# Mish of a unit: one ScalarE instruction in place of sigmoid, tanh seed and one iteration, and the second product one unit sooner

## The chip, the cores and the metric

The kernel runs on one core of a Trainium2 chip. A core has TensorE (PE, with its weight loads shown apart as PEld), VectorE (DVE), ScalarE (ACT), GpSimd (POOL) and SyncE (SP, which issues the DMAs). Each engine takes its instructions in the order in which they were written. The metric is the device time of one execution in microseconds (us), as the median of three runs.

## The reference

Three layers run one after the other on 3072 tokens of width 384. The first is a delta-rule attention, a recurrence over 768 steps. The second is a dense layer of 2048 hidden units with Mish, and the third is a sum over 8 experts of 1024 hidden units, weighted by gates that eight rounds of normalising balance over all tokens.

```python
# attention, per head: y_t = q_t S;  S += beta_t k_t (v_t - S^T k_t)
x = attention(q, k, v, beta)                # 3072 x 384
h = x @ w_in                                # 384 -> 2048
x2 = (h * tanh(log1p(exp(h)))) @ w_out      # Mish, 2048 -> 384
P = balanced(exp(x2 @ w_gate))              # 3072 x 8, eight rounds
out = sum over e of P[:, e] * (relu(x2 @ w1[e]) @ w2[e])
```

## The kernel before, in words

The tokens are cut into six blocks of 512, numbered 0 to 5. After a start of about 111 us, in which the attention of block 0 runs almost alone, there is one window for each block: 16 Mish units (128 hidden units each, f = 0 to 15), then 8 units of the first expert (f = 16 to 23). Into window c is woven the attention of block c+1 (its matrix inverses, and a chain of 16 stages of small products with VectorE work between them) and the preparation of block c+2. After the last window come the other seven experts over all blocks, 336 units of TensorE work to the end of the program.

Every float32 product is made of three passes over a value split in a rounded high part and a low rest. A unit's first product is 9 matmuls into a PSUM bank (`m_first`; two banks of name `psh`). For a Mish unit, `m_a` starts the Mish, `m_b` ends it, `m_x` copies the unit's bank to SBUF (which frees the bank), `m_c` splits the result in `gh` (ScalarE) and `gl` (GpSimd), and `m_second` multiplies both with the second weights, 9 matmuls that add into three banks over all 16 units. `x2_done` reads these banks and splits them as the input of the expert units.

Before the change Mish is made as x (1 - r^2) / (1 + r^2) with r = 1 - sigmoid(x): a Sigmoid and a Tanh on ScalarE give a seed for a reciprocal, three VectorE operations and one of GpSimd prepare an iteration, a Square on ScalarE and two VectorE operations end it. At mark f of a window the code emits `m_first(f)`, `m_b(f-2)`, `m_a(f-1)`, `m_c(f-2)`, `m_x(f-1)`, then side stages, then `m_second(f-3)`; three more marks (f1 to f3) drain the last units, then `x2_done` follows. The two names `s` and `x` of the Mish have two buffers each, and so have `gh` and `gl`.

Side work has its own rules. The order is written out by hand (the table `PLACES` gives the marks). The steps of an inverse lie in a queue `eq` and are taken by VectorE a few at a time: after each VectorE call through the wrapper `vec` (line 461) as far as a credit allows, and by `fill(us)` at fixed places. In block 0 the weights of the Mish layer arrive as 64-bit floats and are decoded there: three VectorE operations a chunk (L191, L194, L199), then a copy on ScalarE (L254) and a subtraction on GpSimd (L255).

Of the kernel before, what the change touches and what calls it, by code (L numbers as in the profile page):

```python
# [8 lines left out]
F32 = mybir.dt.float32  # L9
# [3 lines left out]
AF = mybir.ActivationFunctionType  # L13
# [18 lines left out]
SEED_A, SEED_B = -2.0367336171479424, 0.7523828762448455  # L32
SEED_SHIFT, SEED_SCALE, SEED_ERR = -2.1307765265811733, -0.33690854580335866, 0.0073


def plan_chunks(uses, first, nslots, extra_at, nextra):
    """Which weight chunk goes to which slot, and at which unit it is loaded."""
# [49 lines left out]
def delta_mish_sinkhorn_kernel(  # L87
# [31 lines left out]
    neg3_sb = const.tile([128, 1], F32, name="neg3_sb")  # L119
# [41 lines left out]
    def fetch(i):  # L161
        """Brings a chunk as it is; the first ones of the mish block are 64 bits wide."""
# [20 lines left out]
    def queue_decode(i):  # L183
        """A float64 as a float32: its exponent 896 less, 24 bits of its fraction."""
# [27 lines left out]
    def fill_next():  # L212
        """One step of the side work on the vector engine: its cost, or None if none can be taken."""
        if not eq:
            return None
        cost, fn = eq.popleft()
        fn()
        return cost + 0.001
# [108 lines left out]
    # ================= balanced gates =================  # L327
# [48 lines left out]
    # ================= phase 1: attention and the mish block =================  # L376
# [4 lines left out]
    with ExitStack() as p1:  # L381
# [116 lines left out]
        def prep_ss(c, t):  # L498
            """The same on the scalar engine alone."""
# [12 lines left out]
        def prep_root(c):  # L512
            """Half the norms, from the scalar engine's table; root_ops makes them exact."""
            ss, ne, rn, bn = nrms[c % 2]
            nc.scalar.activation(out=ne, in_=ss, func=AF.Sqrt, scale=0.25)
# [308 lines left out]
        def m_a(u):  # L824
            i = u % 2
            s, p, f = mi_s[i], mi_m[i], mi_f[i]
            nc.scalar.activation(out=s, in_=hps[u], func=AF.Sigmoid)
            nc.scalar.activation(out=f, in_=s, func=AF.Tanh, scale=SEED_A, bias=seed_sb)
            vec.scalar_tensor_tensor(out=p, in0=s, scalar=-2.0, in1=s, op0=ALU.add, op1=ALU.mult)
            vec.tensor_scalar(out=f, in0=f, scalar1=SEED_SHIFT, scalar2=None, op0=ALU.add)  # L830
            vec.scalar_tensor_tensor(out=s, in0=p, scalar=2.0, in1=f, op0=ALU.add, op1=ALU.mult)
            nc.gpsimd.tensor_tensor(out=p, in0=p, in1=f, op=ALU.mult)  # L832

        def m_x(u):
            nc.scalar.activation(out=mi_x[u % 2], in_=hps.pop(u), func=AF.Copy)  # L835

        def m_b(u):
            i = u % 2
            s, p, x = mi_s[i], mi_m[i], mi_x[i]
            nc.scalar.activation(out=s, in_=s, func=AF.Square, scale=2.0 * SEED_SCALE, bias=neg3_sb)  # L840
            vec.scalar_tensor_tensor(
                out=p, in0=s, scalar=3.0 - 3.0 * SEED_ERR ** 2, in1=p, op0=ALU.add, op1=ALU.mult
            )
            vec.scalar_tensor_tensor(
                out=x, in0=p, scalar=-SEED_SCALE / (4.0 - 3.0 * SEED_ERR ** 2), in1=x, op0=ALU.mult, op1=ALU.mult
            )
# [48 lines left out]
        def warm(n, cols=512, i=0):  # L895
            """Keeps the tensor engine's clock up while it waits or its products fill few rows."""
# [13 lines left out]
        with tc.manual_schedule():  # L910
# [20 lines left out]
            nc.vector.memset(seed_sb, SEED_B)  # L931
            nc.vector.memset(half_sb, 0.5)
            nc.vector.memset(neg3_sb, -3.0)
# [30 lines left out]
            nc.scalar.activation(out=mi_s[0][:, 0:1], in_=seed_sb, func=AF.Sigmoid)  # L964
# [82 lines left out]
        def spread(first, last, n, total):  # L1047
            """Places for `total` stages, n at each mark from the first on, and the rest at the last."""
# [16 lines left out]
        def window(c):  # L1065
            """Side work of a window by its place: stages of the tensor engine, and the rest."""
# [46 lines left out]
        with tc.manual_schedule():  # L1113
            banks[:] = [0, [A1, A1]]
            for c in range(NBLK):
# [16 lines left out]
                for f in range(U1 + 3):  # L1132
# [5 lines left out]
                    if 2 <= f < U1 + 2:  # L1138
                        m_b(b + f - 2)
                    if 1 <= f <= U1:  # L1140
                        m_a(b + f - 1)
                    if 2 <= f < U1 + 2:
                        m_c(b + f - 2)
                    if 1 <= f <= U1:
                        m_x(b + f - 1)
# [6 lines left out]
                    if f == 2 or not c:  # L1152
                        banks[1] = [A1, A1, (ps_o1, "o3")]
                    side_rest(m, posts)
                    if 3 <= f:
                        m_second(b + f - 3)
# [7 lines left out]
                x2_done(c)  # L1164
                side_rest("f4", side_pe("f4", 0))
# [175 lines left out]
```

## Time and profile before

| | |
|---|---|
| median of three runs | 2471.75 us (2467.51 to 2473.41) |
| span of the profiled execution | 2464.6 us; no other total of it is shown |
| TensorE busy | 2313.3 us, 94% of the span |
| VectorE busy | 1170.0 us, 47% |
| ScalarE busy | 734.7 us, 30% |
| GpSimd busy | 601.6 us, 24% |
| windows of blocks 0 to 5 | 111.09 to 1047.20 us of the span |

Shares of busy time are means over the start, the windows and the seven experts, which have different limits; so they are read stage by stage. The median lies 7.15 us above the span.

### The profile page before, as it was taken

How to read it: one execution, taken by the hardware profiler on the slowest of the kernel's cores; microseconds unless marked ns; L12 is line 12 of the kernel's file. 1: busy time of each engine (PE TensorE's matmuls, PEld its weight loads, DVE VectorE, ACT ScalarE, POOL GpSimd, SP SyncE). 2: the span in 40 equal slices, each digit the busy share in tenths (PEclk: the TensorE clock that was granted, in tenths of full speed). 3: DMA queues.
4: the chain of work that ended last, by engine and by line, in shares of the span. 5: the costliest groups of instructions: out<-in, count | busy, mean ns of one | idle time of the engine just before them, and what ended most of it. 6: DMA issues, size and time to landing. Idle time of an engine off the chain costs nothing.

```text
span 2464.6 us, 36964 instructions
## 1 busy us (share of the span) xinstructions
PE 2313.3 (94%) x15492; PEld 1995.3 (81%) x15492; DVE 1170.0 (47%) x1850; ACT 734.7 (30%) x1286; POOL 601.6 (24%) x466
## 2 busy tenths in 40 slices
PE   5777989999999998899999999999999999999998
PEld 3556767877778786789999999999999999999998
DVE  8899597877878837642222222222222221222222
ACT  4254455353553535322121121121111112112111
POOL 4675736173460414231020020020001002001000
PEclk8778899999999999999999999999999999999999
DMA  5334752543634444341010010010001001000111
GB/s 166 132 128 151 203 192 105 195 144 142 192 109 168 142 169 164 109 160 39 1 52 1 1 52 1 1 40 13 1 19 34 1 1 52 1 1 26 26 23 29
DMA packets 79734, 196.06 MB, mean 80 GB/s; under 512 B 7696, under 2 KB 50448, under 8 KB 79568
## 3 DMA queue, kind: packets, MB, share of 16 engines
q1 hardware_dynamic: 79568, 193.70, 23.9%
q8 instruction: 122, 2.00, 0.3%
q14 instruction: 44, 0.36, 0.0%
HBM read 161.43 MB, written 32.24 MB: 79 GB/s over the span
## 4 chain that ended last, share of the span: by engine, by line
PE 69%; DVE 13%; POOL 7%; issue 6%; ACT 2%; DMA 1%; SPq 0%; POOLq 0%; DVEq 0%; ACTq 0%
PE psh L302 34%; PE o L324 29%; DVE p L461 3%; PE y L324 3%; POOL p L832 2%; POOL gl L853 2%; DVE x L461 2%; PE x L864 2%; DVE t L638 1%; DVE lane L644 1%; DVE lane L626 1%; POOL w L255 1%; DMA w<-wd 1%; DVE s L461 1%; PE psa L884 1%
## 5 line engine op out<-in xcount | busy, mean ns | idle before, releaser
L317 DVE SCALAR_TENSOR_TENSOR hl<-psh,hh 128x512 fp32r<-128x512 f32 x384 | 265.2, 691 | 1109.7 <-ACT hh L316 1109.6
L302 PE MATMUL psh<-xh,w 128*128 128x512 f32 x2052 | 674.0, 410 | 53.5 <-ACT x L835 29.6
L316 ACT ACTIVATE hh<-psh 128x512 fp32r<-128x512 f32 x384 | 229.7, 598 | 1314.9 <-PE o L324 1152.1
L302 PEld LDWEIGHTS psh<-xh,w 128*128 128x128 f32 x2052 | 387.3, 195 | 138.8 <-ACT x L835 38.0
L302 PE MATMUL psh<-xl,w 128*128 128x512 f32 x1026 | 416.9, 406 | 4.2 <-DVE xl L461 4.2
L324 PE MATMUL o<-w,hh 128*128 128x384 f32 x1584 | 405.3, 337 | 0.0
L324 PEld LDWEIGHTS o<-w,hh 128*128 128x128 f32 x1584 | 288.1, 188 | 19.9 <-issue 5.3
L324 PE MATMUL o<-wx,hh 128*128 128x384 f32 x1104 | 282.4, 336 | 0.0
L324 PE MATMUL o<-w,hl 128*128 128x384 f32 x792 | 266.8, 337 | 0.0
L302 PE MATMUL psh<-xh,wx 128*128 128x512 f32 x828 | 257.5, 392 | 0.0
L302 PEld LDWEIGHTS psh<-xl,w 128*128 128x128 f32 x1026 | 200.1, 195 | 52.0 <-DVE xl L461 6.8
L255 POOL TENSOR_TENSOR w<-raw,w 128x768 fp32r<-128x768 f32 x41 | 76.8, 1872 | 663.6 <-ACT w L254 658.4
L832 POOL TENSOR_TENSOR p<-p,f 128x512 f32<-128x512 f32 x96 | 113.5, 1182 | 446.0 <-DVE s L461 419.0
L324 PEld LDWEIGHTS o<-wx,hh 128*128 128x128 f32 x1104 | 201.7, 188 | 13.0 <-issue 2.2
L324 PE MATMUL o<-wx,hl 128*128 128x384 f32 x552 | 186.1, 337 | 0.0
L302 PEld LDWEIGHTS psh<-xh,wx 128*128 128x128 f32 x828 | 153.4, 188 | 25.0
L864 PE MATMUL x<-gh,w 128*128 128x512 f32 x576 | 157.0, 409 | 7.0 <-ACT gh L852 7.0
L302 PE MATMUL psh<-xl,wx 128*128 128x512 f32 x414 | 163.4, 395 | 0.0
L461 DVE SCALAR_TENSOR_TENSOR p<-s,p 128x512 f32<-128x512 f32 x96 | 122.8, 1279 | 81.2 <-ACT s L840 37.5
L324 PEld LDWEIGHTS o<-w,hl 128*128 128x128 f32 x792 | 148.6, 188 | 0.0
L864 PEld LDWEIGHTS x<-gh,w 128*128 128x128 f32 x576 | 111.6, 197 | 35.7 <-ACT gh L852 10.1
L255 POOL TENSOR_TENSOR wx<-raw,wx 128x768 fp32r<-128x768 f32 x23 | 42.5, 1849 | 398.5 <-ACT wx L254 398.5
(174 smaller groups left out, 3021.5 us busy)
## 6 DMA issues: line engine op xcount, KB each, us to landing
w<-wd SPq DMA_DIRECT2D x120, 768.0 KB, 4.3
raw<-in_w_dram SPq DMA_DIRECT2D x128, 192.0 KB, 2.6
wd<-w SPq DMA_DIRECT2D x24, 768.0 KB, 4.6
kq<-in_qkb_dram SPq DMA_DIRECT2D x20, 256.0 KB, 7.1
vt<-in_vtok_dram SPq DMA_DIRECT2D x6, 768.0 KB, 8.6
kq<-in_w_in_dram SPq DMA_DIRECT2D x12, 384.0 KB, 4.1
kq<-in_w_out_dram SPq DMA_DIRECT2D x12, 384.0 KB, 4.8
y0d<-xr SPq DMA_DIRECT2D x6, 768.0 KB, 4.1
```

The lines of the kernel that those rows point to most:

```text
L255: nc.gpsimd.tensor_tensor(out=w[:, 1], in0=r, in1=w[:, 0].bitcast(F32), op=ALU.subtract)
L302: mm(ps, lhsT=wi(u, pw, kc), rhs=(xh, xl)[px][:, kc, :], start=(n == 0), stop=(n == 3 * KD - 1))
L316: nc.scalar.activation(out=h, in_=ps, func=AF.Relu)
L317: nc.vector.scalar_tensor_tensor(out=l, in0=ps, scalar=0.0, in1=h.bitcast(F32), op0=ALU.max, op1=ALU.subtract)
L324: mm(o[t], lhsT=(h, l)[ph][:, t * 128:(t + 1) * 128], rhs=wo(u, pw, 0, DM), start=(f == 0 and n == 0), stop=(f == U2 - 1 and n == 2))
L461: f(*a, **k)
L626: + [(1.14, lambda p=p: nc.vector.transpose(out=lane[p:p + 32], in_=v[p:p + 32, 32:64, :])) for p in (32, 96)]
L638: eng[0].tensor_tensor(out=slot[0], in0=lane[:, s + 1:32, s:s + 1].to_broadcast([128, n, s]), in1=lane[:, s:s + 1, 0:s].to_broadcast([128, ...
L644: eng[0].tensor_tensor(out=lane[:, s + 1:32, 0:s], in0=lane[:, s + 1:32, 0:s], in1=slot[0], op=ALU.add)
L832: nc.gpsimd.tensor_tensor(out=p, in0=p, in1=f, op=ALU.mult)
L853: nc.gpsimd.tensor_tensor(out=l, in0=p, in1=h.bitcast(F32), op=ALU.subtract)
L864: mm(x2ps[c][k], lhsT=wo(u, pw, k * 128, k * 128 + 128), rhs=(h, l)[pg], start=(f == 0 and n == 0), stop=(f == U1 - 1 and n == 2))
```

## The change

`m_a` becomes one ScalarE instruction, Mish from the activation table, from the PSUM bank to SBUF; this read also frees the bank, so `m_x` goes, and `m_b` with it. `m_c` follows `m_a` at once, at the same mark. `m_second` is emitted two marks after `m_first`, not three, and `x2_done` moves from behind mark f3 to mark f2, ahead of the side stages of f2 and f3. Since fewer calls go through `vec`, a `fill(2.0)` is added at each mark and behind f4. One warming activation at the start loads the Mish table where it loaded that of Sigmoid.

```diff
         def m_a(u):
-            i = u % 2
-            s, p, f = mi_s[i], mi_m[i], mi_f[i]
-            nc.scalar.activation(out=s, in_=hps[u], func=AF.Sigmoid)
-            nc.scalar.activation(out=f, in_=s, func=AF.Tanh, scale=SEED_A, bias=seed_sb)
-            vec.scalar_tensor_tensor(out=p, in0=s, scalar=-2.0, in1=s, op0=ALU.add, op1=ALU.mult)
-            vec.tensor_scalar(out=f, in0=f, scalar1=SEED_SHIFT, scalar2=None, op0=ALU.add)
-            vec.scalar_tensor_tensor(out=s, in0=p, scalar=2.0, in1=f, op0=ALU.add, op1=ALU.mult)
-            nc.gpsimd.tensor_tensor(out=p, in0=p, in1=f, op=ALU.mult)
-
-        def m_x(u):
-            nc.scalar.activation(out=mi_x[u % 2], in_=hps.pop(u), func=AF.Copy)
-
-        def m_b(u):
...
-            nc.scalar.activation(out=s, in_=s, func=AF.Square, scale=2.0 * SEED_SCALE, bias=neg3_sb)
-            vec.scalar_tensor_tensor(
-                out=p, in0=s, scalar=3.0 - 3.0 * SEED_ERR ** 2, in1=p, op0=ALU.add, op1=ALU.mult
-            )
-            vec.scalar_tensor_tensor(
-                out=x, in0=p, scalar=-SEED_SCALE / (4.0 - 3.0 * SEED_ERR ** 2), in1=x, op0=ALU.mult, op1=ALU.mult
-            )
+            nc.scalar.activation(out=mi_x[u % 2], in_=hps.pop(u), func=AF.Mish)
...
-            nc.scalar.activation(out=mi_s[0][:, 0:1], in_=seed_sb, func=AF.Sigmoid)
+            nc.scalar.activation(out=mi_s[0][:, 0:1], in_=seed_sb, func=AF.Mish)
...
-                    if 2 <= f < U1 + 2:
-                        m_b(b + f - 2)
                     if 1 <= f <= U1:
                         m_a(b + f - 1)
-                    if 2 <= f < U1 + 2:
-                        m_c(b + f - 2)
-                    if 1 <= f <= U1:
-                        m_x(b + f - 1)
+                        m_c(b + f - 1)
...
+                    if f == U1 + 1:
+                        m_second(b + U1 - 1)
+                        x2_done(c)
                     side_rest(m, posts)
-                    if 3 <= f:
-                        m_second(b + f - 3)
+                    if 2 <= f <= U1:
+                        m_second(b + f - 2)
+                    fill(2.0)
...
-                x2_done(c)
                 side_rest("f4", side_pe("f4", 0))
+                fill(2.0)
```

Where the instructions stand is seen at three places. The first is TensorE at the start of block 5, in which no side work lies. L302 (L299 after the change) is a first product, and the number behind `w` is its weight slot; L864 (L840) is a second product into the banks `x`. Before, from the third unit of the block on:

```order
L302 MATMUL psh<-xh_1200,w_88 128x512 x2
L302 MATMUL psh<-xl_1201,w_88 128x512
...
L302 MATMUL psh<-xh_1200,w_89 128x512 x2
L302 MATMUL psh<-xl_1201,w_89 128x512
...
L864 MATMUL x_8636<-gh,w_86 128x512
L864 MATMUL x_8637<-gh,w_86 128x512
```

And with the change, from the same unit on:

```order
L299 MATMUL psh<-xh_1198,w_87 128x512 x2
L299 MATMUL psh<-xl_1199,w_87 128x512
...
L840 MATMUL x_7878<-gh,w_85 128x512
L840 MATMUL x_7879<-gh,w_85 128x512
...
L299 MATMUL psh<-xh_1198,w_88 128x512 x2
L299 MATMUL psh<-xl_1199,w_88 128x512
```

The second product of unit 0 (slot 86 before, 85 now) stood behind the first product of unit 3 and stands now behind that of unit 2.

The second place is ScalarE in block 5. Before, two units take these rows, where L827 is Sigmoid, L828 Tanh, L840 Square, L852 the split into `gh`, L835 the copy that frees the bank:

```order
L827 ACTIVATE s_172<-psh 128x512
L828 ACTIVATE f_178<-s_172,seed_sb 128x512
L852 ACTIVATE gh<-x_177 128x512
L835 ACTIVATE x_176<-psh 128x512
L840 ACTIVATE s_172<-s_172,neg_sb 128x512
L827 ACTIVATE s_173<-psh 128x512
```

Now the last units of block 5 read as follows, where L822 is Mish, L828 the split, L846 and L852 are `x2_done`, L313 is a Relu of an expert unit, and L344 the Sigmoid of the gates:

```order
L822 ACTIVATE x_175<-psh 128x512
L828 ACTIVATE gh<-x_175 128x512
L822 ACTIVATE x_176<-psh 128x512
L828 ACTIVATE gh<-x_176 128x512
L846 ACTIVATE xh_1198<-x_7878 128x512
...
L852 ACTIVATE xr<-x_7880 128x512
L313 ACTIVATE hh<-psh 128x512
L344 ACT_TABLE_LOAD
L344 ACTIVATE lg<-lg,gate 128x192
```

A unit has two ScalarE instructions, not five. The program before has three table loads, all in the start; the program after has the same three and this fourth, and none among the Mish units.

The third place is GpSimd in block 0, where it also prepares keys and values (L549, L563) and splits decoded weights (L255). Before, one mark of the block reads:

```order
L832 TENSOR_TENSOR p_175<-p_175,f_179 128x512
L853 TENSOR_TENSOR gl<-x_176,gh 128x512
L549 TENSOR_TENSOR vt_145<-vt_145,ne_153 128x384
L563 TENSOR_TENSOR kq_139<-kq_139,mask_sb 64x512
L255 TENSOR_TENSOR w_86<-kq_136,w_86 128x768
```

And with the change, the mark with the same work:

```order
L829 TENSOR_TENSOR gl<-x_176,gh 128x512
L546 TENSOR_TENSOR vt_144<-vt_144,ne_152 128x384
L560 TENSOR_TENSOR kq_138<-kq_138,mask_sb 64x512
L252 TENSOR_TENSOR w_85<-kq_135,w_85 128x768
L829 TENSOR_TENSOR gl<-x_175,gh 128x512
```

The product of the iteration (L832) is gone, the low part of a unit is made one mark sooner, and what else stands in the queue ahead of it stays.

## Rows read from the trace of the kernel before

**Rows 1.** The page, part 2: the span in 40 slices, tenths busy; granted clock.

```profile
DVE  8899597877878837642222222222222221222222
...
PEclk8778899999999999999999999999999999999999
```

**Rows 2.** Stretches: us, busy us and instructions of PE PEld DVE ACT POOL, PEclk, DMA, GB/s.

```profile
111.09:267.03 155.94, 117.42 (x1121) 90.01 (x1121) 141.30 (x159) 76.60 (x124) 102.34 (x76) 0.81 0.47 154
133.24:202.48 69.24, 50.39 (x557) 39.14 (x557) 67.96 (x69) 35.93 (x55) 44.88 (x29) 0.77 0.42 137
202.48:246.96 44.48, 36.84 (x411) 29.73 (x411) 42.55 (x50) 20.55 (x33) 27.10 (x17) 0.89 0.42 144
246.96:267.03 20.07, 15.37 (x49) 10.40 (x46) 13.78 (x17) 10.43 (x21) 12.78 (x9) 0.74 0.76 199
267.03:316.06 49.03, 47.34 (x321) 41.18 (x321) 29.75 (x63) 17.95 (x35) 30.81 (x30) 0.93 0.73 240
316.06:473.64 157.58, 140.02 (x1391) 115.15 (x1390) 130.61 (x235) 74.02 (x130) 69.20 (x57) 0.97 0.46 152
473.64:780.57 306.93, 284.60 (x2780) 233.40 (x2778) 249.13 (x418) 147.87 (x260) 138.03 (x114) 0.96 0.46 152
780.57:914.77 134.20, 130.57 (x1200) 107.67 (x1198) 90.96 (x125) 65.83 (x110) 39.14 (x32) 0.96 0.44 154
914.77:1005.16 90.39, 74.76 (x303) 55.35 (x302) 64.00 (x84) 50.79 (x85) 38.74 (x32) 0.98 0.45 158
1005.16:1047.20 42.04, 40.77 (x208) 35.23 (x209) 29.75 (x79) 10.16 (x18) 5.68 (x3) 0.96 0.25 85
1047.20:2464.60 1417.40, 1407.50 (x7061) 1271.81 (x7060) 337.51 (x542) 247.15 (x395) 115.47 (x58) 1.00 0.08 25
```

**Rows 3.** The same view of single units: block 4, block 5, and an expert unit.

```profile
847.77:853.17 5.40, 5.40 (x54) 4.31 (x50) 4.51 (x8) 3.17 (x5) 2.42 (x2) 1.00 0.41 149
965.95:971.26 5.31, 4.45 (x18) 3.30 (x18) 3.96 (x6) 3.05 (x5) 2.42 (x2) 1.00 0.48 148
894.79:898.95 4.16, 4.16 (x22) 3.79 (x22) 0.69 (x1) 0.60 (x1) 0.00 (x0) 1.00 0.51 189
```

**Rows 4.** Groups by line, whole run: busy us, mean ns, idle before and its releasers.

```profile
L461 DVE SCALAR_TENSOR_TENSOR p<-s,p 128x512 f32<-128x512 f32 x96 | 122.8, 1279 | 81.2 <-ACT s L840 37.5 <-POOL p L832 31.0 <-POOL kq L563 6.7
...
L461 DVE SCALAR_TENSOR_TENSOR x<-p,x 128x512 f32<-128x512 f32 x96 | 87.2, 909 | 3.2
...
L461 DVE SCALAR_TENSOR_TENSOR p<-s 128x512 f32<-128x512 f32 x96 | 78.2, 815 | 5.3 <-ACT s L827 5.3
...
L461 DVE SCALAR_TENSOR_TENSOR s<-p,f 128x512 f32<-128x512 f32 x96 | 66.4, 692 | 3.2
...
L827 ACT ACTIVATE s<-psh 128x512 f32<-128x512 f32 x96 | 56.7, 590 | 18.4 <-PE psh L302 17.5
...
L461 DVE TENSOR_SCALAR f<-f 128x512 f16<-128x512 f16 x96 | 29.0, 302 | 0.1
```

**Rows 5.** Timeline of VectorE (DVE) in block 0: start us, length us, instruction, idle before.

```profile
124.12 0.67 DVE L461 SCALAR_TENSOR_TENSOR p<-s,p 128x512 f32<-128x512 f32 x1
...
129.04 1.77 DVE L461 SCALAR_TENSOR_TENSOR p<-s,p 128x512 f32<-128x512 f32 x1 [1.85 <-POOL p L832]
```

**Rows 6.** Timeline of GpSimd (POOL) in the same stretch.

```profile
127.84 1.16 POOL L832 TENSOR_TENSOR p<-p,f 128x512 f32<-128x512 f32 x1
128.96 1.30 POOL L853 TENSOR_TENSOR gl<-x,gh 128x512 fp32r<-128x512 f32 x1
```

**Rows 7.** Timeline of ScalarE at the table load before the units.

```profile
21.05 1.28 ACT L964 ACT_TABLE_LOAD   x1
```

**Rows 8.** Timeline at the end of the Mish units of block 5.

```profile
1001.87 0.63 ACT L852 ACTIVATE gh<-x 128x512 fp32r<-128x512 f32 x1 [3.08 <-DVE x L461]
...
1002.55 1.66 PE L864 MATMUL x<-gh,w 128*128 128x512 f32 x6 [1.03 <-ACT gh L852]
...
1005.16 0.73 PE L302 MATMUL psh<-xh,w 128*128 128x512 f32 x2 [0.23 <-ACT xh L870]
```

More of the change, by code (lines that the diff above doesn't have):

```diff
@@ L31 @@
 ROUNDS = 8
-SEED_A, SEED_B = -2.0367336171479424, 0.7523828762448455
-SEED_SHIFT, SEED_SCALE, SEED_ERR = -2.1307765265811733, -0.33690854580335866, 0.0073
 def plan_chunks(uses, first, nslots, extra_at, nextra):
@@ L118, in delta_mish_sinkhorn_kernel @@
     seed_sb = const.tile([128, 1], F32, name="seed_sb")
-    neg3_sb = const.tile([128, 1], F32, name="neg3_sb")
     lg = const.tile([128, NT, E], F32, name="lg")
@@ L824, in m_a @@
         def m_a(u):
-            i = u % 2
-            s, p, f = mi_s[i], mi_m[i], mi_f[i]
-            nc.scalar.activation(out=s, in_=hps[u], func=AF.Sigmoid)
-            nc.scalar.activation(out=f, in_=s, func=AF.Tanh, scale=SEED_A, bias=seed_sb)
-            vec.scalar_tensor_tensor(out=p, in0=s, scalar=-2.0, in1=s, op0=ALU.add, op1=ALU.mult)
-            vec.tensor_scalar(out=f, in0=f, scalar1=SEED_SHIFT, scalar2=None, op0=ALU.add)
-            vec.scalar_tensor_tensor(out=s, in0=p, scalar=2.0, in1=f, op0=ALU.add, op1=ALU.mult)
-            nc.gpsimd.tensor_tensor(out=p, in0=p, in1=f, op=ALU.mult)
-        def m_x(u):
-            nc.scalar.activation(out=mi_x[u % 2], in_=hps.pop(u), func=AF.Copy)
-        def m_b(u):
-            i = u % 2
-            s, p, x = mi_s[i], mi_m[i], mi_x[i]
-            nc.scalar.activation(out=s, in_=s, func=AF.Square, scale=2.0 * SEED_SCALE, bias=neg3_sb)
-            vec.scalar_tensor_tensor(
-                out=p, in0=s, scalar=3.0 - 3.0 * SEED_ERR ** 2, in1=p, op0=ALU.add, op1=ALU.mult
-            )
-            vec.scalar_tensor_tensor(
-                out=x, in0=p, scalar=-SEED_SCALE / (4.0 - 3.0 * SEED_ERR ** 2), in1=x, op0=ALU.mult, op1=ALU.mult
-            )
+            nc.scalar.activation(out=mi_x[u % 2], in_=hps.pop(u), func=AF.Mish)
         def m_c(u):
@@ L930, in delta_mish_sinkhorn_kernel @@
             nc.gpsimd.memset(mi_f[1], 0.0)
-            nc.vector.memset(seed_sb, SEED_B)
+            nc.vector.memset(seed_sb, 0.0)
             nc.vector.memset(half_sb, 0.5)
-            nc.vector.memset(neg3_sb, -3.0)
             nc.vector.memset(sk["ones"], 1.0)
```

## The prediction

> **What bounds the kernel now.** I read the slices of the page first. VectorE is mostly at 7 to 9 tenths through the first sixteen slices and at 2 after the nineteenth, and the granted TensorE clock shows a 7 or an 8 only in the first five [rows 1]. So I cut the span at the starts of the blocks [rows 2]. From 1047.20 us on, in the other seven experts, TensorE is busy 1407.5 of 1417.4 us at full clock, and no edit touches that code; the start up to 111 us loses one memset. What can change lies in 936.1 us of windows, of which TensorE is busy 835.5. Its 100.6 us of idle time, and what it works at half clock, are the stock to gain from.
>
> The stock lies unevenly. In the Mish part of block 0 TensorE is idle 38.5 of 155.9 us at a granted clock of 0.81, while VectorE is busy 141.3. In block 5's Mish part it is idle 15.6 of 90.4, in block 1 17.6 of 157.6, in blocks 2 and 3 together 22.3 of 306.9, in block 4 only 3.6 of 134.2 [rows 2]. Single units say why. A unit of block 4 with one side stage takes 5.40 us without any idle time: TensorE is the bound. A bare unit of block 5 takes 5.31 us with 0.86 idle, and no engine is full: there the latency of the Mish is the bound. An expert unit, as many matmul columns, takes 4.16 [rows 3]. So a bare Mish unit needs about 4.35 of TensorE (4.45 less a little, since busy time counts waits inside a group), and a side stage 5.40 - 4.35 = 1.05.
>
> **What each edit costs or gives.** Five VectorE instructions go: 1279 + 909 + 815 + 692 + 302 ns = 4.0 us a unit, 384 us over 96 units [rows 4]. The GpSimd product of 1.16 us goes too [rows 6], and three ScalarE instructions. Mish itself has no row. The Sigmoid that reads the same bank at the same shape takes 590 ns [rows 4]; an activation of that shape lies between this and the 630 ns of the split into `gh` [rows 8], or higher if Mish needed more per element. I take 0.6. Even 1.2 would be less than what ScalarE loses, since that engine is busy only 3.05 of 5.31 us of a bare unit [rows 3].
>
> *Block 0, units 4 to 9.* They take 69.24 us, 11.5 each, with VectorE busy 67.96 [rows 2]. These busy times hold waiting. The same instruction takes 0.67 us alone [rows 5], and 1.77 where the GpSimd subtraction of 1.30 us ran from 128.96 on [rows 5, 6]: it ended 0.55 us after that. So the two engines shut each other out, and their times add. The Trainium skill says so of the port pair that VectorE and GpSimd share ("SBUF — State Buffer", SBUF: two separate sides): an exclusive lock, held for the whole instruction, against which a two-input VectorE operation blocks. The trace agrees with 1.77 against 0.67 us. If the times did not add, block 0 would fall at once to TensorE's need. With them added, a unit loses the free lengths, four operations at 0.69 (the row with the least waiting in rows 4) and one at 0.30, and the GpSimd product at 1.16: 4.2 us. That leaves 7.3 a unit, above TensorE's need of about 6.2 (4.35 and nearly two stages), because the decoding and the splitting of weights stay. 6 x 7.3 = 44: **25 less**.
>
> *Units 10 to 14* take 44.48, 8.9 each; less 4.2 is 4.7, which is below TensorE's 4.35 + 2 x 1.05 = 6.45. I take 6.7: **11 less**. *The end of the block*, from the last first product to the expert units, takes 20.07 [rows 2]: four second products, and between them the whole latency of the last Mish. With the second product one unit sooner, one first product (2.2), three second products (6.5) and 2 us of hand-over remain: 10.7, **9.4 less**; the fourth second product is made earlier in the block, where it costs 2.2, but a wait of some 1.2 beside it goes: **1 more**. Block 0's Mish part: **44 less**, 156 to 112.
>
> *The expert units of block 0* take 49.03 with 1.7 idle and a clock of 0.93, which costs up to 0.07 x 49 = 3.4: they come out of a stall before them, and I take **3.5 less**.
>
> *Blocks 1 to 4.* Idle time plus (1 - clock) x length is the most to be won: block 1 17.6 + 4.7 = 22.3, blocks 2 and 3 22.3 + 12.3 = 34.6, block 4 3.6 + 5.4 = 9.0 [rows 2]. The units in mid-block are already full [rows 3]; the loss lies at the end of the Mish units and where the chain of the next block begins, and both wait on the VectorE queue or on the Mish latency. What remains is the hand-over in `x2_done` (now partly under the stages of f2 and f3, which stand behind it) and the first stages of the inverse, 4 to 6 us a block. I take **16, 27 and 4 less**.
>
> *Block 5, Mish part.* 15.6 idle and 0.02 x 90.4 = 1.8 of clock; 1.5 of hand-over stays: **16 less**. The last second product waited 1.03 us on `gh`, itself 3.08 late by VectorE, and the expert units after `x2_done` waited only 0.23 and ran slowly behind it [rows 8].
>
> *What is added.* One table load of 1.28 us [rows 7] ahead of the gates' Sigmoid, once, off TensorE's way by one unit: 0 to 1.3, I take 0. The `fill(2.0)` calls move work of the queue `eq` forward, and add none. In blocks without queued steps they do nothing.
>
> Sum: 44 + 3.5 + 16 + 27 + 4 + 16 = 110.5. The profiled execution would span 2464.6 - 110.5 = 2354.1 us. The median of the runs stands 7.15 above its span, so the forecast is 2471.75 - 110.5, **2361 us**.
>
> **What the sooner second product asks for.** It adds a possible wait: TensorE is in order, and behind a late `gl` stand the next first products, and behind those the whole window. From the end of `m_first(u)` to `m_second(u)` there lie two second and two first products, 4 x 2.17 = 8.7 us. In that time come Mish 0.6, split 0.63, subtraction 1.30, some 3 us with hand-overs. The third place of the order shows what GpSimd does between two subtractions in block 0: three or four pieces of 1 to 2 us. This fits with little to spare there, and with 4 us or more elsewhere, where GpSimd is busy 2.42 us a unit [rows 3].
>
> **The rivals.**
> *All floors reached* (1 in 10). VectorE and GpSimd no longer meet, block 0 falls to TensorE's need (units 4 to 9 at 6.2, 32 less; 12; 9.4; 1 more: 52 less), the others lose all their stock, 3.5 + 22.3 + 34.6 + 9.0 + 17.4: 139 less, **2333 us**. Against it speaks the decoding left in block 0.
> *GpSimd becomes the bound* (13 in 100). It keeps 27 to 45 us of work in those 44 to 69 us of block 0 [rows 2], it still shuts VectorE out, and half of the stock of blocks 1 to 4 is chain latency that no Mish caused. Block 0 gives 15 and 2, blocks 1 to 4 24, block 5 16: 57 less, **2415 us**.
> *Slower: the second product stalls on `gl`* (2 in 100). Place: each `m_second`, through the GpSimd queue. To eat the 110 us it must cost 1.15 us in each of 96 units, so `gl` must come 9.8 us after its first product, 7 late. GpSimd would have to be nearly full; it is busy 102 of 156 us in block 0 and under half elsewhere [rows 2]. If it lost 1.5 a unit: 144 - 110 is 34 slower, **2506 us**.
> *The change is not what it says: Mish needs a table of its own* (2 in 100), so that each unit pays two loads of 1.28 [rows 7], for Mish and for the copies. ScalarE would go to 3.05 - 2.0 + 2.56 = 3.6 of 4.35 us a unit, mostly hidden; block 0, where it is busy 76.6 of 155.9, would lose perhaps 10 and the rest 10: **2385 us**. The Trainium skill ("ScalarE: Activation LUTs", Table sets: the hidden batching unit) says that tables come in named sets and that a switch between sets is paid each time, which would speak against this change. The second place of the order shows no load among the units.
>
> **How the numbers follow.** The forecast has 71 in 100, with its own range 2346 to 2384 (block 0 between 30 and 50 less, the others two thirds to nearly all of their stock, Mish up to 1.2 us). For 8 in 10 the range reaches into the first two rivals, about half way into each, since their times spread as well (12 of their 23 in 100): **2336 to 2410**. A difference under 0.3% can't be told from none here (7 us; the three runs span 6). The stall, and 2 in 100 for what I have not thought of, end at or above no change: slower 0.03, same 0.01, faster 0.96.
>
> **What would show it.** After: no VectorE instruction of line 461 that reads `s` or `p`; TensorE's idle time in the windows down from 100 to about 30 us; the Mish part of block 0 near 112 us and still with VectorE and GpSimd blocking each other; block 5's units at 4.3 to 4.4 us instead of 5.31; mid-block units of blocks 1 to 4 unchanged; the last 1417 us unchanged. The prediction is wrong if the second products wait on `gl`, if a Mish takes well over 0.7 us, or if block 0 stays above 130 us.

## The result, and the profile after the change

The changed kernel takes 2372.58 us (median of 4 runs, 2370.98 to 2375.13) against 2471.03 us before in the same comparison: ratio 0.9604, 95% interval 0.9591 to 0.9618. The forecast was 2361 us, the range 2336 to 2410. The profiled execution spans 2369.2 us, 95.4 less than before; it took 2370.98 us.

The slices of the page, as in [rows 1]:

```profile
DVE  8884725527162104431222222222222122212222
...
PEclk6799999999999999999999999999999999999999
```

VectorE is at 7 tenths or more in five slices, where it was in fourteen, and the clock is low only in the first two. The same stretches as in [rows 2], cut at the new starts of the blocks (us, busy us and instructions of PE, PEld, DVE, ACT, POOL, PEclk, DMA share, GB/s):

```profile
110.19:217.19 107.00, 96.33 (x1121) 77.75 (x1121) 76.83 (x77) 48.45 (x74) 78.56 (x59) 0.92 0.63 212
131.68:176.99 45.31, 39.06 (x557) 31.60 (x555) 40.68 (x33) 22.23 (x33) 38.62 (x23) 0.92 0.64 214
176.99:208.43 31.44, 31.44 (x415) 25.82 (x411) 20.63 (x24) 14.24 (x21) 18.96 (x12) 1.00 0.69 230
208.43:217.19 8.76, 8.53 (x41) 6.68 (x37) 1.04 (x3) 3.94 (x8) 3.15 (x2) 1.00 0.63 192
217.19:276.35 59.16, 51.48 (x320) 44.30 (x321) 30.84 (x65) 18.75 (x37) 33.40 (x30) 0.86 0.70 216
276.35:427.69 151.34, 141.79 (x1391) 117.62 (x1390) 73.68 (x157) 44.19 (x82) 45.36 (x41) 0.94 0.48 160
427.69:710.58 282.89, 276.60 (x2780) 228.74 (x2778) 124.66 (x256) 87.56 (x164) 89.80 (x82) 0.98 0.50 166
710.58:839.34 128.76, 128.53 (x1200) 106.32 (x1198) 29.26 (x44) 36.34 (x62) 20.49 (x16) 0.99 0.45 160
839.34:908.82 69.48, 69.25 (x303) 56.13 (x301) 1.82 (x4) 21.73 (x37) 20.64 (x16) 1.00 0.57 198
908.82:949.59 40.77, 39.57 (x208) 34.51 (x209) 29.79 (x79) 11.45 (x19) 5.63 (x3) 1.00 0.30 102
949.59:2369.20 1419.61, 1409.79 (x7061) 1272.41 (x7060) 337.44 (x542) 247.15 (x395) 115.35 (x58) 1.00 0.08 25
```

TensorE's idle time in the windows is now 839.4 us of windows less 803.6 busy: 36 us, where it was 100.6. Block 0's Mish part fell by 49 us. Its expert units, the fifth row, grew from 49.03 to 59.16 us at a clock of 0.86: time was given back there.

The two Mish units, with a side stage (block 4) and bare (block 5), which answer to [rows 3]:

```profile
775.69:781.13 5.44, 5.44 (x54) 4.32 (x50) 0.56 (x1) 1.23 (x2) 1.27 (x2) 1.00 0.44 149
866.65:870.86 4.21, 4.21 (x20) 3.39 (x19) 0.00 (x0) 1.24 (x3) 1.29 (x1) 1.00 0.53 189
```

The first is as long as it was, the second shorter by 1.1 us and now the length of its matmuls. What held a bare unit of block 5 before was the round of the Mish itself (VectorE prepares a unit, GpSimd multiplies, VectorE ends the unit and only then begins the next), and it reached TensorE through the bank and not through the second product: 10.9 of TensorE's 15.6 us of idle time there are 13 waits for `m_x` (L835), the copy that frees the bank of the next first product and stands on ScalarE behind the split of the unit before. VectorE waited 14 times, 17.0 us in all, for the GpSimd product of the same unit, with no other work between. Two rows of one unit before (start us, length us, instruction, idle before):

```profile
987.17 0.72 PE L302 MATMUL psh<-xh,w 128*128 128x512 f32 x2 [0.87 <-ACT x L835]
988.73 1.77 DVE L461 SCALAR_TENSOR_TENSOR p<-s,p 128x512 f32<-128x512 f32 x1 [1.28 <-POOL p L832]
```

Over 118 to 1110 us of the span before, these waits for the copy are TensorE's largest, 29.6 us in 21. Both causes go with the change: Mish's own read frees the bank, and no VectorE operation is left in a unit.

Groups by line on ScalarE (busy us, mean ns, idle before and its releasers) price the new instruction at 597 ns, beside the split into `gh`:

```profile
L828 ACT ACTIVATE gh<-x 128x512 fp32r<-128x512 f32 x96 | 60.6, 632 | 61.7 <-PE x L840 61.0
L822 ACT ACTIVATE x<-psh 128x512 f32<-128x512 f32 x96 | 57.3, 597 | 168.3 <-PE psh L299 167.9
```

What TensorE waits for between 111 and 1000 us (us in total, times, longest):

```profile
PE psh L299 <- DMA w<-wd: 6.7, 1, 6.7
PE psa L590 <- issue: 5.5, 1, 5.5
PE psh L299 <- DVE xl L458: 4.2, 1, 4.2
PE psa L729 <- DVE r L458: 4.1, 1, 4.1
```

These are the four largest; no second product (L840) stands among the others either, and so `gl` is nowhere late. The two longest waits have nothing to do with Mish. The first expert unit of block 0 shows the second of them. SyncE's queue, then TensorE, then GpSimd (start us, length us, instruction, idle before):

```profile
219.72 0.33 SPq L854 DMA_DIRECT2D x2d<-xr  x1
220.09 0.43 SPq L468 DMA_DIRECT2D kq<-in_qka_dram  x1
...
224.66 0.54 SPq L469 DMA_DIRECT2D kq<-in_qkb_dram  x1
```

```profile
225.27 0.65 PE L590 MATMUL psa<-kq 48*64 48x128 f32 x2 [5.47 <-issue]
```

```profile
221.21 5.45 POOL L507 TENSOR_TENSOR ne<-ss,half_sb 128x32 f32<-128x32 f32 x1 [6.87 <-DVE ss L491]
```

Eight loads of block 2's keys and queries stand in SyncE's queue behind the store of `x2_done`, which waits for `xr`. The first is issued at 220.09, the quickest of these loads lands 5.1 us after its issue, and the key product starts at 225.27. The profile names no releaser for it (`issue`), but the times fit the landing of the first load. The GpSimd power of 5.45 us, which the key scaling needs, also starts only after `x2_done` has gone through VectorE.

The longest wait stands in block 1. SyncE, then TensorE:

```profile
282.77 0.32 SPq L810 DMA_DIRECT2D y0d<-xr  x1
283.14 0.42 SPq L468 DMA_DIRECT2D kq<-in_qka_dram  x1
...
288.41 3.73 SPq L245 DMA_DIRECT2D w<-wd  x4
```

```profile
290.44 0.85 PE L840 MATMUL x<-gl,w 128*128 128x512 f32 x3
297.95 1.19 PE L299 MATMUL psh<-xh,w 128*128 128x512 f32 x2 [6.66 <-DMA w<-wd]
```

The weights of the next first product are issued behind a store and eight loads, and TensorE waits 6.66 us for them. The kernel before had the same wait at the same place:

```profile
339.79 1.19 PE L302 MATMUL psh<-xh,w 128*128 128x512 f32 x2 [6.04 <-DMA w<-wd]
```

### The profile page after: what moved, and what is told of

It reads as the page before. It is cut to its first block, busy times and chain, and to the rows that moved or that the text cites. A ratio compares the mean times of both kernels' runs of the same rounds, so it can differ in the third digit from the quotient of the medians.

```text
span 2369.2 us, 36112 instructions
## 1 busy us (share of the span) xinstructions
PE 2298.2 (97%) x15492; PEld 1992.1 (84%) x15492; DVE 801.2 (34%) x1369; ACT 559.9 (24%) x999; POOL 471.2 (20%) x370
## 4 chain that ended last, share of the span: by engine, by line
PE 90%; DVE 6%; DMA 2%; POOL 1%; issue 1%; ACT 0%; SPq 0%; DVEq 0%; POOLq 0%; ACTq 0%
PE psh L299 42%; PE o L321 30%; PE x L840 8%; PE y L321 3%; DVE t L635 1%; DVE lane L641 1%; PE psa L590 1%; PE psa L729 1%; PE psa L763 1%; DVE lane L623 1%; PE psa L711 1%; PE psa L860 1%; PE psa L747 1%; PE psa L677 1%; DMA wd<-w 0%
## 5 line engine op out<-in xcount | busy, mean ns | idle before, releaser
L299 PE MATMUL psh<-xh,w 128*128 128x512 f32 x2052 | 662.7, 404 | 13.7 <-DMA w<-wd 6.7
L313 ACT ACTIVATE hh<-psh 128x512 fp32r<-128x512 f32 x384 | 229.7, 598 | 1312.1 <-PE o L321 1154.5
L299 PEld LDWEIGHTS psh<-xh,w 128*128 128x128 f32 x2052 | 381.1, 191 | 91.2 <-issue 12.2
L299 PE MATMUL psh<-xl,w 128*128 128x512 f32 x1026 | 412.0, 402 | 4.2 <-DVE xl L458 4.2
L299 PE MATMUL psh<-xh,wx 128*128 128x512 f32 x828 | 258.3, 393 | 0.0
L299 PEld LDWEIGHTS psh<-xl,w 128*128 128x128 f32 x1026 | 196.3, 191 | 51.2 <-DVE xl L458 5.9
L829 POOL TENSOR_TENSOR gl<-x,gh 128x512 fp32r<-128x512 f32 x96 | 127.5, 1328 | 420.0 <-ACT gh L828 416.2
L252 POOL TENSOR_TENSOR w<-raw,w 128x768 fp32r<-128x768 f32 x41 | 75.7, 1848 | 669.9 <-ACT w L251 669.8
L299 PEld LDWEIGHTS psh<-xh,wx 128*128 128x128 f32 x828 | 153.5, 188 | 25.2
L299 PE MATMUL psh<-xl,wx 128*128 128x512 f32 x414 | 163.4, 395 | 0.0
L840 PE MATMUL x<-gh,w 128*128 128x512 f32 x576 | 150.7, 397 | 0.0
L840 PEld LDWEIGHTS x<-gh,w 128*128 128x128 f32 x576 | 107.5, 189 | 24.9
L252 POOL TENSOR_TENSOR wx<-raw,wx 128x768 fp32r<-128x768 f32 x23 | 42.4, 1845 | 399.7 <-ACT wx L251 399.7
L321 PEld LDWEIGHTS o<-wx,hl 128*128 128x128 f32 x552 | 103.6, 188 | 0.0
```

Source lines behind the costliest of these rows:

```text
L252: nc.gpsimd.tensor_tensor(out=w[:, 1], in0=r, in1=w[:, 0].bitcast(F32), op=ALU.subtract)
L299: mm(ps, lhsT=wi(u, pw, kc), rhs=(xh, xl)[px][:, kc, :], start=(n == 0), stop=(n == 3 * KD - 1))
L313: nc.scalar.activation(out=h, in_=ps, func=AF.Relu)
L321: mm(o[t], lhsT=(h, l)[ph][:, t * 128:(t + 1) * 128], rhs=wo(u, pw, 0, DM), start=(f == 0 and n == 0), stop=(f == U2 - 1 and n == 2))
L829: nc.gpsimd.tensor_tensor(out=l, in0=p, in1=h.bitcast(F32), op=ALU.subtract)
L840: mm(x2ps[c][k], lhsT=wo(u, pw, k * 128, k * 128 + 128), rhs=(h, l)[pg], start=(f == 0 and n == 0), stop=(f == U1 - 1 and n == 2))
```

## The experiments

Theory A, from the prediction: the gain is the VectorE and GpSimd work that goes (block 0) and the latency that goes (block 5); the sooner second product adds little. Its rival: part of the gain, or the loss in block 0's expert units, comes from the order. In the tables below, "Mish" is from the first product of unit 0 to that of unit 16, "experts" from there to the next block, in us of the profiled execution.

### The two halves of the change

**e1_mish_alone**: the new Mish in the order of before.

```diff
                     if 1 <= f <= U1:
                         m_a(b + f - 1)
-                        m_c(b + f - 1)
+                    if 2 <= f < U1 + 2:
+                        m_c(b + f - 2)
...
-                    if f == U1 + 1:
-                        m_second(b + U1 - 1)
-                        x2_done(c)
                     side_rest(m, posts)
-                    if 2 <= f <= U1:
-                        m_second(b + f - 2)
+                    if 3 <= f:
+                        m_second(b + f - 3)
...
+                x2_done(c)
                 side_rest("f4", side_pe("f4", 0))
```

> The changed kernel with its one-instruction Mish, but the split one mark later, the second product three marks behind the first and the hand-over to the expert units behind mark f3, as before the change. Theory A (nearly all of the 98 us comes from the shorter Mish; the sooner second product is worth a hand-over of a few us a block, and costs block 0 about as much in its expert units, because the hand-over now stands ahead of the key loads and the power): 2366 to 2390 us, block 0's expert units back near 49 us, bare units of block 5 at 4.2 us. Theory B (the sooner second product is worth a whole unit, 4.3 us, in each of six blocks): 2395 us or more.

**e2_sooner_alone**: the Mish of before with the sooner second product and `x2_done` (`m_c` stays where it was).

> The kernel before, with its long Mish, with the second product two marks behind the first and the hand-over at f2. Theory A: the long Mish, about 10 us from the end of the first product to the low part, does not fit in the 8.7 us that are left, so TensorE waits for it in each unit: bare units of block 5 between 5.5 and 8 us instead of 5.31, the whole 2480 to 2560 us, slower than before. Theory B (the latency of the Mish is hidden either way): within 10 us of the kernel before, or faster.

| us | total, ratio (interval) | block 0 Mish, experts | block 1 Mish | Mish of blocks 2, 3, 4 | block 5 Mish |
|---|---|---|---|---|---|
| before | 2471.03 | 155.94, 49.03 | 118.45 | 112.50, 112.49, 97.14 | 90.39 |
| after | 2372.58, 0.9604 (0.9591 to 0.9618) | 107.00, 59.16 | 113.25 | 101.96, 105.66, 91.52 | 69.48 |
| e1 | 2372.55, 0.9609 (0.9595 to 0.9623) | 108.66, 46.95 | 109.27 | 106.69, 109.08, 96.11 | 69.43 |
| e2 | 2481.36, 1.0053 (1.0037 to 1.0069) | 154.85, 58.70 | 124.14 | 113.23, 114.19, 97.99 | 91.48 |

Mish in the old order gives the whole gain. e1 holds three things, the shorter Mish, the bank freed by Mish's own read, and the `fill(2.0)` calls; no run takes these apart. The new order costs 12 us in block 0's experts and 4 in block 1, and wins 3 to 5 in each of blocks 2 to 4: nothing in sum (the intervals of e1 and of the change overlap). Put on the old Mish it is a loss of half a per cent, with the same 10 us in block 0's experts. e2's total lies just inside the range of theory A, but by luck. The waits in each unit came: in block 5's Mish part 15 second products wait 14.2 us for `gl`. They came in place of the waits for the bank, which are gone, and VectorE still waits 1.28 us a unit for the GpSimd product. So a bare unit takes 5.28 us, as before and not 5.5 to 8, and block 5's Mish part grew by 1 us only.

### Load or latency

**e3_load_kept**: the changed kernel with six operations of the removed kinds on scratch tiles in `m_a`; no product waits for their results. **e12_vector_kept** keeps the five of VectorE alone, **e13_gpsimd_kept** the one of GpSimd alone.

```diff
+            s, p, f = mi_s[0], mi_m, mi_f
+            for _ in range(4):
+                nc.vector.scalar_tensor_tensor(out=p[0], in0=s, scalar=-2.0, in1=s, op0=ALU.add, op1=ALU.mult)
+            nc.vector.tensor_scalar(out=f[0], in0=f[1], scalar1=0.5, scalar2=None, op0=ALU.add)
+            nc.gpsimd.tensor_tensor(out=p[1], in0=s, in1=s, op=ALU.mult)
```

> The changed kernel with the removed work put back beside the path: in each Mish unit four two-input operations and one 16-bit operation on VectorE and one product on GpSimd, at the old shapes, on scratch buffers that nothing reads. The output is that of the changed kernel. Theory A (in block 0 the gain is the time that VectorE and GpSimd hold each other up; elsewhere it is the latency of the Mish): block 0's Mish part goes from 107 to 140 us or more, blocks 1 to 5 stay within 8 us, whole 2405 to 2440 us. Theory B (latency alone, everywhere): within 10 us of the changed kernel, 2365 to 2383 us.

> The changed kernel, with five VectorE operations of the removed kinds and shapes on scratch tiles in each Mish unit, and without the GpSimd product; nothing waits for their results. With both kept on scratch, the Mish units of block 0 took 154.9 us, against 107.0 without. Theory H (VectorE and GpSimd shut each other out, so the times of all six add, the step of the prediction): the five give 3.06 of 4.22 us a unit of the free lengths, so block 0's Mish units lie at about 142 us, total 2430 to 2455. Rival I (VectorE alone is the bound, and the GpSimd product lies beside it): 152 to 155 us in block 0, total 2460 to 2470.

> The changed kernel with only the GpSimd product of each Mish unit kept on a scratch tile; nothing waits for its result. Theory H: 1.16 of 4.22 us a unit, block 0's Mish units at about 118 to 121 us, total 2383 to 2400. Rival I: block 0 within 2 us of 107.0, total 2371 to 2376.

| us | total, ratio (interval) | block 0 Mish | block 5 Mish, experts |
|---|---|---|---|
| after | 2372.58, 0.9604 (0.9591 to 0.9618) | 107.00 | 69.48, 40.77 |
| e13, GpSimd's kept | 2379.17, 0.9632 (0.9612 to 0.9652) | 113.41 | 69.48, 42.60 |
| e12, VectorE's kept | 2424.31, 0.9815 (0.9796 to 0.9835) | 147.45 | 69.48, 42.16 |
| e3, both kept | 2468.76, 0.9994 (0.9984 to 1.0004) | 154.86 | 69.48, 53.79 |

Block 0's Mish part by its stages, cut as in [rows 2]:

| us | units 0 to 3 | units 4 to 9 | units 10 to 14 | end |
|---|---|---|---|---|
| before | 22.15 | 69.24 | 44.48 | 20.07 |
| after | 21.49 | 45.31 | 31.44 | 8.76 |
| e13 | 21.34 | 51.87 | 31.44 | 8.76 |
| e12 | 21.29 | 72.07 | 45.34 | 8.75 |
| e3 | 21.61 | 76.13 | 48.36 | 8.76 |

In units 4 to 14 the load is everything: they take 117.4 us with VectorE's part kept and 124.5 with both, against 113.7 before, although no result is waited for. The end keeps its gain of 11.3 us in each of these runs, so load is not what it paid for. That e3's block 0 is as long as before is the sum of the two. The parts add: 40.5 and 6.4 make 46.9, and both together cost 47.9. That VectorE alone is the bound (rival I) is out. H's prices do not hold either. VectorE's five operations cost 4.5 us a unit in units 4 to 9, not the 3.06 of their free lengths. GpSimd's product costs its length there (6.6 us for six of 1.16) and nothing from unit 10 on, where TensorE is busy all 31.44 us: 6.4 us in all, not 11 to 14. Nor does e13 show that the product holds VectorE up. The two rows are units 4 to 9 of e12 and of e13, columns as in [rows 2]:

```profile
134.59:206.66 72.07, 45.17 (x557) 36.21 (x555) 70.25 (x66) 22.29 (x33) 39.89 (x24) 0.76 0.43 146
135.53:187.40 51.87, 40.59 (x557) 32.52 (x555) 41.27 (x32) 22.31 (x33) 47.30 (x32) 0.90 0.55 184
```

In e12 VectorE is full. In e13 GpSimd is nearly full (47.30 of 51.87), and in these units TensorE waits 6.6 us for weights that GpSimd splits (L252), against 2.1 after the change. Block 0 with VectorE's part kept lies between the two theories, e13's total too, and e12's total is below both.

In block 5 the load costs the Mish units nothing, so their gain of 21 us is not load but the round of the Mish. With both kept 13.0 us come back in the expert units behind them, with VectorE's part alone 1.4; so of block 5's 22.2 us 9.2 are left in e3.

e3's total lies beyond what theory A gave for it, and blocks 1 to 5 did not stay within 8 us. Of the 96.8 us by which its span exceeds that of the changed kernel, 47.9 lie in block 0's Mish part, 1.1 in its experts, 39.8 in blocks 1 to 5, 1.2 in the last stretch, and 6.9 in the start, which no edit touches (113.3 to 117.1 us in e3, e4, e12 and e13, 110.2 to 112.0 in the others; the cause is open). So it is chance that the total is that of the kernel before. Windows of block 0's Mish units and block 5's experts in e3, and TensorE's longest waits in its windows:

```profile
117.10:271.96 154.86, 109.99 (x1120) 87.64 (x1120) 147.38 (x149) 48.54 (x74) 103.20 (x75) 0.81 0.44 147
991.40:1045.19 53.79, 44.69 (x207) 38.97 (x208) 37.40 (x93) 11.56 (x19) 5.62 (x3) 0.84 0.23 79
```

```profile
PE psh L299 <- DVE xl L458: 21.2, 5, 7.8
PE psh L299 <- DMA w<-wd: 16.4, 3, 10.1
PE psa L729 <- DVE r L458: 16.4, 2, 11.3
PE psa L677 <- DVE t L650: 10.0, 1, 10.0
```

The weights (`w<-wd`) are late in blocks 1 to 3, by 10.1, 3.3 and 3.0 us, where after the change one such wait of 6.7 stands in block 1. VectorE's timeline at the end of block 5's Mish units in e3 says why its experts are late:

```profile
991.01 2.15 DVE L825 SCALAR_TENSOR_TENSOR p<-s 128x512 f32<-128x512 f32 x3
...
999.24 1.88 DVE L458 TENSOR_TENSOR xl<-x,xh 128x512 fp32r<-128x512 f32 x3
```

VectorE is behind by more than two units of scratch work, and `x2_done` (`xl`) stands in its queue behind that. So in block 5 load costs nothing inside a unit, and is paid at the next place where something needed comes behind it.

The Trainium skill ("SBUF — State Buffer", SBUF: two separate sides) names an exclusive lock on the ports that VectorE and GpSimd share. The trace agrees in kind: a kept operation of VectorE with two inputs (L825) takes 1392 ns on the mean in units 4 to 9 of e12, beside GpSimd's work, and four of them 2.86 us, 715 ns each, at the end of block 5 in e3, where GpSimd is idle. One operation need not follow this: between 131 and 209 us the decoding operation L191 takes 1680 ns after the change, 2125 in e13, and 1106 in e3.

**e14_mish_twice** computes each Mish twice in a row on ScalarE.

```diff
+            nc.scalar.activation(out=mi_m[0], in_=hps[u], func=AF.Mish)
             nc.scalar.activation(out=mi_x[u % 2], in_=hps.pop(u), func=AF.Mish)
```

> The changed kernel with the Mish of each unit computed twice in a row, the first time into a scratch tile, so that it costs ScalarE 1.2 us a unit and comes 0.6 us later. The prediction's step (a Mish of up to 1.2 us costs next to nothing, since the slack from a first product to its second product covers it): total 2370 to 2378, bare units of block 5 at 4.19 us. Rival J (the latency of Mish still counts, above all in block 0): 0.6 us in each unit of block 0 and at each end of a block, 10 to 15 us, total 2382 to 2388.

It took 2374.32 us, ratio 0.9614 (0.9596 to 0.9632). A bare unit of block 5 in its windows:

```profile
868.32:872.52 4.20, 4.20 (x20) 3.38 (x19) 0.00 (x0) 1.72 (x4) 1.29 (x1) 1.00 0.58 190
```

The unit is as long as with one Mish, and the total's interval overlaps that of the change: a Mish of 1.2 us would have cost nothing that can be measured, and its 597 ns is off the path.

### Why block 0's experts and block 1 are late

Theory B: the store and the loads behind it, two of the four squares, and the power all stand behind `x2_done`; each alone keeps the stages late. **e4_store_late** issues the store behind f4.

```diff
-            if c < NBLK - 1:
-                nc.sync.dma_start(out=x2_dram[c], in_=xr)
...
                 side_rest("f4", side_pe("f4", 0))
+                x2_store(c)
```

> The changed kernel with the store of the block's Mish output to DRAM issued behind the stages of f4 instead of at the hand-over, so that the key loads of block 2 no longer stand behind it in the queue of SyncE. Theory A (the 10 us lost in block 0's expert units are these late key loads): the key loads start at about 213 us of the span instead of 220, block 0's expert units take 50 to 53 us instead of 59.2, the whole 2362 to 2367 us. Theory B (the squares and the power on GpSimd, which also stand behind the hand-over, are as late, so that TensorE only waits for them instead): the wait of 5.5 us before the first key product goes, but block 0's expert units stay above 56 us and the whole above 2369 us.

It took 2370.32 us, ratio 0.9604 (0.9588 to 0.962); block 0's experts took 58.52. The wait of the key product is gone, and the next unit waits instead, as theory B has it:

```profile
233.37 5.29 PE L862 MATMUL psa<-wg_sb,xr 128*128 128x8 f32 x24 [6.01 <-ACT kq L555]
```

**e7_both_early** moves the loads four marks and the squares and power two marks forward in window 0. **e8_kq_late1** moves the loads of window 1 behind the weights.

```diff
-            (5, spread(5 + 3, 26, 2, 16), 21 - 5,
-             [21 - 2, 21 - 1, 21, 21 + 1], spread(21, 27, 2, 8), 18, 26, 24),
+            (5, spread(5 + 3, 26, 2, 16), 21 - 7,
+             [21 - 2, 21 - 1, 21, 21 + 1], spread(21, 27, 2, 8), 14, 26, 24),
```

```diff
-             [8 - 2, 8 - 1, 8 + 1, 8 + 3], spread(8, 19, 1, 8), 1, 27, 19),
+             [8 - 2, 8 - 1, 8 + 1, 8 + 3], spread(8, 19, 1, 8), 5, 27, 19),
```

> The changed kernel, but in window 0 the loads of block 2's keys and queries are issued four marks sooner, and its squares and GpSimd power two marks sooner, so that neither stands behind x2_done. Issuing the store late moved the wait from the first expert unit to the second and gave nothing. Theory B (store, squares and power all stand behind x2_done, each alone makes the next stage late): the expert units of block 0 fall from 59.2 to about 49 us, as before the change; total 2362 us, ratio about 0.956. Rival C (these units are late since the stages of the chain themselves are bunched there, whatever is prepared): they stay at 56 to 60 and the total at 2371 to 2374, or the loads moved into the full part of block 0 make its Mish units longer by as much.

> The changed kernel, but in window 1 the loads of keys and queries are issued at mark 5, not 1, so that the second weights of the Mish unit stand ahead of them in the SyncE queue. Theory D (the stall of 6.7 us at the start of block 1 is that weight load behind the store of the first layer's result and eight loads; it is no wait of the Mish): the stall goes, the Mish units of block 1 take 106 to 109 us, not 113.2, total 2366 us, ratio about 0.958. Rival E (the weight load is late because of the store alone, or the later keys make the masks and the chain late): the Mish units of block 1 stay within 2 us of 113, total 2371 to 2374.

e7: 2365.76 us, ratio 0.9583 (0.957 to 0.9596); block 0's experts 50.52, its Mish part 110.08. Theory B holds for these units; 8.6 us come back and 3.1 are lost where the pieces now lie. The squares and the power were not moved without the loads. e8: 2365.66 us, 0.9577 (0.9562 to 0.9592); block 1's Mish part 110.50, only 2.7 less. It loses the DMA wait, but the unit behind it takes 12.70 us, of which TensorE waits 4.0 at the first small product of the chain (L677), so D is half right, and its total of 2366 us was met by luck: another 3.5 us came in block 3 (102.12), which the edit does not touch. After the change and in e7, e10, e11 and e14 block 3's Mish part takes 105.7 to 106.3 us, and TensorE has one wait of 2.9 to 3.9 us there, at L712; in e8 one of 2.0 at L711 stands in its place. The profile names no releaser for either, so what decides it is open.

### A better order

**e10_order_by_block** takes the order of before in blocks 0 and 1 and the new one in blocks 2 to 5 (`lag = int(c < 2)`). **e11_both** adds e8's edit.

```diff
+                    lag = int(c < 2)
                     if 1 <= f <= U1:
                         m_a(b + f - 1)
-                        m_c(b + f - 1)
+                    if 1 + lag <= f <= U1 + lag:
+                        m_c(b + f - 1 - lag)
...
-                    if f == U1 + 1:
+                    if f == U1 + 1 and not lag:
...
-                    if 2 <= f <= U1:
-                        m_second(b + f - 2)
+                    if 2 + lag <= f <= U1 + 2 * lag:
+                        m_second(b + f - 2 - lag)
...
+                if lag:
+                    x2_done(c)
```

> The changed kernel's Mish, with the order of before (second product three marks behind, x2_done behind f3) in blocks 0 and 1, and the new order in blocks 2 to 5. With the Mish alone the order of before gave 108.7 and 47.0 us in block 0, 109.3 and 37.6 in block 1; the new order gave 102.0, 105.7 and 91.5 in the Mish units of blocks 2 to 4, against 106.7, 109.1 and 96.1. Theory F (the two orders gain and lose in different blocks, and these differences add): 2357 us, 15 less than the changed kernel, ratio about 0.954. Rival G (the differences only move a delay from one block to the next): 2369 to 2374, ratio 0.959 to 0.961.

> The order by block as in the run before, and the loads of keys and queries of window 1 at mark 5. Theories D and F together: the gains add, about 2351 us, ratio 0.951; block 1's Mish units about 104. Rival E or G: as that run without it, within 2 us.

e10: 2356.99 us (2355.34 to 2362.68), ratio 0.9548 (0.9534 to 0.9562), below the changed kernel's interval: the best of these kernels, and what theory F gave. Its block 0 and block 1's Mish part:

```profile
111.16:219.98 108.82, 97.42 (x1120) 77.86 (x1120) 78.04 (x79) 47.44 (x76) 80.10 (x60) 0.92 0.62 208
219.98:266.97 46.99, 44.59 (x320) 38.92 (x321) 29.65 (x63) 17.98 (x35) 31.24 (x30) 1.00 0.88 284
266.97:376.24 109.27, 101.02 (x1199) 81.30 (x1197) 41.46 (x81) 37.25 (x71) 45.16 (x41) 0.97 0.42 134
```

The experts of block 0 run at full clock again. e11: 2360.00 us, 0.9556 (0.9542 to 0.957), no better. Its block 1 Mish part is 104.63, as expected, but the spans are 2354.8 and 2355.1: the 4.6 us won there are lost again, 2.2 in block 2's Mish part, 1.5 in block 4's experts, 1.1 in the last stretch and the rest in the start and block 0, while block 5's experts win 1.4. Why is open.

## Why the prediction came out as it did

The forecast lay 11.6 us under the result by the medians, and 15.1 by the spans (2354.1 against 2369.2). Luck hides the difference: the profiled execution before lay 7.15 us under its median, that after the change only 3.4. By the spans:

| term | predicted, us | measured |
|---|---|---|
| block 0, units 4 to 9 | -25 | 69.24 to 45.31: -23.9 |
| units 10 to 14 | -11 | 44.48 to 31.44: -13.0 |
| end of its Mish units | -9.4 | 20.07 to 8.76: -11.3 |
| the earlier second product, in units 0 to 3 | +1 | 22.15 to 21.49: -0.7 |
| block 0, expert units | -3.5 | 49.03 to 59.16: **+10.1** |
| block 1 | -16 | 157.58 to 151.34: **-6.2** |
| blocks 2 and 3 | -27 | 306.93 to 282.89: -24.0 |
| block 4 | -4 | 134.20 to 128.76: -5.4 |
| block 5, Mish | -16 | 90.39 to 69.48: -20.9 |
| block 5, experts; the rest; the start | 0 | -1.3; +2.2; -0.9 |

**Right.** The larger part is Mish and not the order (e1). Load on VectorE and GpSimd held block 0's units 4 to 14 (e3, e12), and the latency of the Mish a bare unit of block 5 (e3). Mish costs 0.60 us as taken, and 1.2 would have been free (e14). The table is loaded once before the gates, not among the units. Mid-block units with a stage did not change, and the second product waits on `gl` nowhere: none of the four rivals came. The nearest by time, a table load in each unit, is ruled out by the order of the instructions; its own terms, 10 and 10 above the forecast, give 2381 us and not 2385. GpSimd as the bound is near in units 4 to 9, where it is busy 38.62 of 45.31 us, and e13 prices its whole product at 7 us of the total (2379.17).

**Right in its sum, not shown in its step: the times add.** The sum of free lengths, 4.2 us a unit, agrees with what units 4 to 9 lost, 23.9 us in six. But the same operations on scratch tiles cost 30.8 us there, since VectorE's take longer than their free lengths, and what GpSimd's product adds alone (e13) goes through GpSimd's own queue. That VectorE's operations take longer beside GpSimd's work is shown (1392 against 715 ns); that the cost is the sum of the free lengths is not.

**The step that failed: block 0's expert units.** I took 3.5 us less, since they "come out of a stall before them", and set the moved `x2_done` down as a help in the hand-over. I did not count what it was moved past. It puts a store ahead of eight loads in SyncE's queue, and its VectorE and ScalarE work ahead of two of the squares, on which a GpSimd power of 5.45 us waits. The units took 10.1 us more. e1 and e10 take them to 47 us with the old order, e2 gives 59 with the old Mish, e4 shows that the store alone is not it, and e7 (50.52), that loads, squares and power together are most of it.

**The step that was mis-sized: block 1.** I set down all its idle time as VectorE queue or Mish latency. 6 us of it were a weight load that came late in SyncE's queue, before and after alike; I had not asked for the waits of that block. What e8 won shows that part of it could not be had by moving the loads alone. Another 4 us are the new order: with the old one the Mish part takes 109.27 us, not 113.25 (e1).

**Sizes.** These misses are partly made up by others of the opposite sign. The bare Mish unit needs 4.2 us of TensorE, not 4.35, and all of block 5's hand-over went: nearly 5 us more than forecast. Where the prediction looked at waits of second products on `gh`, TensorE waited in the main for the bank. The end of block 0's Mish units I put down to the sooner second product. In e1, with the old order, that stretch takes 11.80 us, not 20.07: most of it was the length of the Mish, and the sooner second product only moves 2 to 3 us to another place.

**Not accounted for.** The last stretch took 2.2 us more (1419.61 against 1417.40) with the same matmuls and clock. It takes 1419.6 to 1421.4 us in every kernel here with the new Mish, 1417.4 and 1414.5 in the two with the old one (before and e2), so it belongs to the change; why is open.

## What to carry to other kernels

Before a step is moved, list what then stands behind it on every engine, SyncE's queue and the slow GpSimd operations included: here the new order cost in two blocks what it won in three, and the best version chose the order by block. Idle time of a block is to be split by its waits before it is put down to the work that goes: the waits name the copy that frees a bank, or a weight load, where one thinks of latency. When work is removed, ask of each stage whether it paid for load or for latency. The same work kept on scratch tiles answers it if it is read stage by stage; the total of such a run can meet that of the kernel before by chance.

## What the runs showed of the hardware

- Mish from the table takes 597 ns at 128x512 from PSUM, about as long as Sigmoid did (590 in [rows 4]), and copies, Relu, squares and the split into `gh` run between the Mish of two units without a table load. The gates' Sigmoid takes one of 1.28 us, as the order showed. In the start after the change a load (L512) runs from 6.88 to 8.16 us, between an activation that ends at 6.86 and one that begins at 8.17: nothing is paid there beyond the load. The Trainium skill ("ScalarE: Activation LUTs", Table sets: the hidden batching unit) says that cheap functions are in every set and that a change of set is paid. The trace agrees: no load for Copy and Relu among the Mish units, one of 1.28 us for the Sigmoid.
- A GpSimd product of 1.16 us a unit cost block 0 6.4 us over 16 units alone, and 7.4 on top of the kept VectorE work (154.86 against 147.45). Alone it cost 1.1 us a unit where GpSimd was nearly full (units 4 to 9) and nothing where TensorE was. A VectorE operation with two inputs took 715 ns with GpSimd idle and 1392 beside its work.
- Where TensorE stalled in block 0's expert units, the granted clock fell to 0.86 on the mean; without the stall it is 1.00 (e10). By that share an estimated 8 of the 59 us at most are clock (0.14 of 59.16), more than the stall of 5.47; two matmuls of a first product that take 0.73 us at 217.19 take 1.22 at 230.03.
